# Strided heads of blocks 3 to 5 begun in the last two chunks of the block two back, and the transposes, norm and input of each block asked for one to two chunks sooner

## Chip, cores and metric

The kernel runs on one core of a Trainium2 chip. The metric is the device time of one execution in microseconds (us); the median of three runs is compared. The core's engines work side by side, each in the order of its own queue: TensorE (PE in the profile, its weight loads PEld), VectorE (DVE), ScalarE (ACT), GpSimd (POOL) and SyncE (SP), which here only starts DMA transfers.

## The reference, cut to what matters

Attention over 4 sequences of 576 positions with 8 heads of 64, then two gated feed-forward layers. Four heads are local (each query sees the 32 last keys), four are strided (each query sees the earlier keys with the same position modulo 32).

```python
scores = scale * np.matmul(q, k.transpose(0, 1, 3, 2))
mask_local = (rel >= 0) & (rel < stride)                      # heads 0 to 3
mask_strided = (rel >= 0) & (pos[None, :] % stride == pos[:, None] % stride)   # heads 4 to 7
attn = softmax(where(mask, scores, -1e9)); x = attn @ v       # 2304 tokens x 512
xn = x / sqrt(mean(x*x) + 1e-6) * rms_g                       # first layer, 512 -> 1536 -> 512
x = (silu(xn @ w_gate) * (xn @ w_val)) @ w_out
out = ((x @ w_a) * (x @ w_b)) @ w2_out                        # second layer, the same sizes
```

## The kernel before

**Blocks and chunks.** The 2304 tokens are cut into six blocks of 384 (96 positions of each sequence), `t` = 0 to 5. The first layer runs block by block. Inside a block the 1536 hidden channels are cut into twelve chunks of 128, `fc` = 0 to 11. A chunk is 12 matmuls for the gate (`g_ps`), 12 for the value (`v_ps`) and 12 for the output of the chunk before (`y`); each product is made of three matmuls, of a high and a low part of both operands (L475 to L477). Between them ACT makes `sg` (Silu, L737), DVE `h` = `sg` times the value (L747), ACT the high part of `h` (L489) and POOL or DVE its low part (L490). The second layer follows the sixth block and is not touched.

**Attention beside it.** While block `t` is on PE, the attention of block `t + 1` is worked out by the other engines, in steps that `attention_slot` (L600) asks for after each chunk's gate matmuls. The steps of the strided heads need no PE. `lq` (L209) loads the queries `qs_t` and sets the score tile `S`; `ls0` to `ls3` load the keys of a head into a `kv` buffer (L217); `sqk<head><row>` multiplies on POOL (L232) and sums on DVE (L235); `ssub`, `sexp`, `snorm` are the softmax; `lv0` to `lv3` load the values; `spv<head><row>` multiplies on POOL (L265) and sums on DVE (L268) into `xs_t`. Then `xst0` and `xst1` turn `xs_t` around on PE (L388), `xstc` copies the result on ACT (L397), `sq2` and `sq3` square it (L409) and add the squares (L415). `rms` sums the squares with a matmul (L421), `rinv` takes the root (L425) and the reciprocal on DVE (L427), and `xp0` to `xp3` make the block's input: `xn` on DVE (L433), its high part on ACT (L437) and its low part on DVE for blocks 2 and 4 and on POOL for blocks 1, 3 and 5 (L438). These are the operands of the next block's first matmuls.

**Which chunk asks for what.** The list of strided steps has 42 entries for blocks 2 to 5: `lq`, 16 for the scores, 3 for the softmax, 16 for the values, and the six `xst0 xstc0 xst1 xstc1 sq2 sq3`. It is spread evenly over chunks 0 to 9; `rms` and `rinv` are asked for in chunk 10 and the four `xp` in chunk 11. The local heads have a list of their own (`LOCAL`, L51): `qk` on PE (L280), then mask (L298), maximum (L307), exponential (L317 or L320), norm, transposes and values.

**Who sets the order.** Steps are emitted in program order, and the compiler's planner then orders each engine's queue by that priority and by its own estimate of when an instruction is ready. An engine that the planner sees idle takes later work early. What holds work back is a buffer: `qs_t` and `xs_t` share one buffer (tag `qx`, `bufs=1`), `S` has one, `kv` has three, `prod` two.

**Block 5.** Beside block 5 there is no attention to make. Its place in SBUF is taken by the forms of the second layer's weights (`convert_forms`): raw halves are loaded (L106), decoded by ACT and DVE (L129, L134, L137), split into high and low parts by ACT and POOL (L142, L143), summed (L656 to L659) and stored. The tiles of this pool lie over those of the attention's pool, so the first raw loads wait for the last reader there.

```python
for fc in range(NFC):
    ...                                    # gate and value matmuls of chunk fc of block t
    if nxt is not None:
        attention_slot(nxt, fc)            # steps of block t + 1
    if prev is not None:
        emit_y(*prev)                      # output matmuls of the chunk before
```

Of the kernel before, what the change touches and what calls it, by code (L numbers as in the profile page):

```python
# [10 lines left out]
F32 = mybir.dt.float32  # L11
# [7 lines left out]
B, H, S, D = 4, 8, 576, 64  # L19
# [3 lines left out]
NB = S // PB  # L23
NTB = B * PB
NM = S // W
NFC = FF // 128
NCC = DM // 128
# [27 lines left out]


FUSED = ["  F", "   ", "   ", "F  ", "FFF", "FFF"]
# [17 lines left out]
def fused_kernel(ctx: ExitStack, tc: tile.TileContext, qtl, ktl, vl, qs, ks, vs, cst, w1, w2, out):  # L75
# [79 lines left out]
    def run(steps):  # L155
        for f in steps:
            f()
# [13 lines left out]
    def attention(t, pool, psum, banks):  # L171

        L = 3 * (t + 1)
        G = {0: 4, 1: 2}.get(t, 1)
        KX, KB = (12 * D, 2) if t < 2 else (NM * D, 3)
        st = {}
        steps = {}

# [27 lines left out]
        def heads(g):  # L206
            return slice(g * G, g * G + G)

        def load_q():  # L209
            q_t = pool.tile([128, 4, 3, D], F32, tag="qx", name="qs_t", bufs=1)  # L210
            nc.sync.dma_start(q_t, qs[:, :, 3 * t:3 * t + 3, :])
            st["qs"] = q_t
            st["S"] = pool.tile([128, 4, 3, 6 if t < 2 else NM], F32, tag="S", name="S_t", bufs=1)
            nc.vector.memset(st["S"], NEG)

        def load_kv(src, key, g):
# [7 lines left out]
        def product(n):  # L224
            pr = pool.tile([128, KX], F32, tag="prod", name="prod", bufs=2)
            return pr[:, :G * n * D].rearrange("p (g n d) -> p g n d", g=G, d=D)
# [32 lines left out]
        def spv(g, mm):  # L259
            def f():  # L260
                n = 3 * t + mm + 1
                if "xs" not in st:
                    st["xs"] = pool.tile([128, 3, 4, D], F32, tag="qx", name="xs_t", bufs=1)
                pr = product(n)
                st["pvm"] = nc.gpsimd.tensor_tensor(  # L265
                    pr, st["vs", g][:, :, :n, :],
                    st["S"][:, heads(g), mm, :n, None].to_broadcast([128, G, n, D]), op=ALU.mult)
                st["pvr"] = nc.vector.tensor_reduce(st["xs"][:, mm, heads(g), :],  # L268
                                                    pr.rearrange("p g n d -> p g d n"), axis=X, op=ALU.add)
            return f  # L270
# [194 lines left out]
        qk_steps = [f"sqk{g}{mm}" for g in range(ng) for mm in range(3)]  # L465
        pv_steps = [f"spv{g}{mm}" for g in range(ng) for mm in range(3)]
        for lst, ld in ((qk_steps, "ls"), (pv_steps, "lv")):
            for g in reversed(range(ng)):
                lst.insert(max(0, 3 * (g - 1)), f"{ld}{g}")
        steps["strided"] = ["lq"] + qk_steps + ["ssub", "sexp", "snorm"] + pv_steps + ["xst0", "xstc0", "xst1", "xstc1", "sq2", "sq3"]  # L470
        return steps


# [5 lines left out]
    def mm_in(ps, w, sel, x):  # L479
        for cc in range(NCC):  # L480
            c = slice(cc * 128, (cc + 1) * 128)
            mm3(ps, w[:, sel, 0, c], w[:, sel, 1, c], x[cc][:, 0], x[cc][:, 1], cc == 0, cc == NCC - 1)
# [13 lines left out]
    psum = one.enter_context(tc.tile_pool(name="psum", bufs=1, space=bass.MemoryType.PSUM))  # L496
# [11 lines left out]
    pool = apool.enter_context(tc.tile_pool(name="early", bufs=1))  # L508
# [15 lines left out]
    def load_late(which):  # L524
        raw.update(zip(which, load_pair(w1, which, pool)))
# [67 lines left out]
    def load_wo(t, fc):  # L593
        wt = wo[t, fc] = wo_tile()
        nc.sync.dma_start(wt.rearrange("p a n -> p (a n)").bitcast(F32), wod[fc])


    local = [dict(enumerate(order.split("|"))) for order in LOCAL]

    def attention_slot(steps, fc):  # L600
        st = steps["strided"]
        n_sl = 10
        part = st[len(st) * fc // n_sl:len(st) * (fc + 1) // n_sl] if fc < n_sl else []
        part += local[min(t, 1)].get(fc, "").split()
        part += ["rms", "rinv"] * (fc == n_sl) + [f"xp{cc}" for cc in range(4)] * (fc == n_sl + 1)
        for n in part:
            steps[n]()


# [69 lines left out]
    def x_forms(g):  # L679

        b = {}

        def load():
            for n, (j, (t, k)) in enumerate({"11": (0, 0), "12": (1, 0), "22": (1, 1), "21": (0, 1)}.items()):
                b[j] = slab[n // 2][:, n % 2 * 2 * NTB:(n % 2 + 1) * 2 * NTB].rearrange("p (c n) -> p c n", c=2)
                nc.sync.dma_start(b[j], x2d[2 * g + t, k])

        def form(p, src):
            f = xf[p] = slab[FORM_SLAB[p]][:, :4 * NTB].rearrange("p (a c n) -> p a c n", a=2, c=2)
            parts(src, f[:, 0], f[:, 1], nc.gpsimd if p in (3, 4, 7) else nc.vector)  # L690

        def less(dst, x, y):
            nc.vector.tensor_tensor(b[dst], b[x], b[y], op=ALU.subtract)


        return {1: [load],
                2: [lambda: form(1, b["11"]), lambda: less("11", "12", "11")],
                5: [lambda: form(5, b["11"]), lambda: less("12", "22", "12"), lambda: less("11", "22", "11"),
                    lambda: form(6, b["11"]), lambda: form(2, b["21"])],
                6: [lambda: form(7, b["12"])],  # L700
                7: [lambda: form(3, b["22"])],
                8: [lambda: less("21", "21", "11"), lambda: form(4, b["21"])]}

    x0 = x_forms(0)
    prev = None
    for t in range(NB):
        if t == 1:
            apool.close()
            pool = apool.enter_context(tc.tile_pool(name="attn", bufs=1))
        if t == NB - 1:  # L710
            apool.close()
            cpool.close()
            pool = p2.enter_context(tc.tile_pool(name="forms", bufs=1, reuse_waits="tile"))
            early = [f for k in (4, 5, 0, 1, 2, 3) for f in convert_forms(k, k < 4)]
        nxt = attention(t + 1, pool, psum, itertools.cycle(["att"])) if t + 1 < NB else None
        x = [xt[t, cc] for cc in range(NCC)]
        for fc in range(NFC):
            if t > 0 and fc == 0:
                load_wo(t, 0)
            g_ps = psum.tile([128, 512], F32, tag="gv", name="g_ps", bufs=3)  # L720
            mm_in(g_ps[:, :NTB], gv[fc], 0, x)
            v_ps = psum.tile([128, 512], F32, tag="gv", name="v_ps", bufs=3)
            mm_in(v_ps[:, :NTB], gv[fc], 1, x)
            if t == 0 and fc + 1 < NFC:
                with gate(fc + 1):
                    convert1(fc + 1)
                if fc + 2 == NFC:
                    load_late([(NFC - 2, 2), (NFC - 1, 2)])
            if t == NB - 1:
                slab[fc] = wgt.tile([128, 4 * DM], F32 if fc in (0, 1, 11) else F32R, tag="gv", name="slab", bufs=NFC)  # L730
                run(early[len(early) * fc // NFC:len(early) * (fc + 1) // NFC])
                for k in [k for k in x0 if k <= fc]:
                    run(x0.pop(k))
            sg = tmp("sg")
            if t == 0:
                nc.vector.tensor_tensor(sg, g_ps[:, :NTB], ri0, op=ALU.mult)
            nc.scalar.activation(sg, sg if t == 0 else g_ps[:, :NTB], AF.Silu)  # L737
            if fc == 1 and t > 0:
                evac_y(t - 1)
            if nxt is not None:  # L740
                attention_slot(nxt, fc)
            if prev is not None:
                emit_y(*prev)
            if t > 0 and fc + 1 < NFC:
                load_wo(t, fc + 1)
            h = tmp("h")
            nc.vector.tensor_tensor(h, sg, v_ps[:, :NTB], op=ALU.mult)  # L747
            hl[t, fc] = split(h, engine(HLO0[fc] if t == 0 else HLO[t]))
            if t == 0:
                wt = wo[0, fc] = wo_tile()  # L750
                with gate(fc + 1):
                    run(conversion(raw.pop((fc, 2)), wt, pool, engine(WLO[fc][2]), LOW[fc][2]))
                nc.sync.dma_start(wod[fc], wt.rearrange("p a n -> p (a n)").bitcast(F32))
                if fc % 2:
                    load_units(1)
                if fc == NFC - 3:
                    load_late([(NFC - 1, 0), (NFC - 1, 1)])
            prev = (t, fc)
# [7 lines left out]
    psum = p2.enter_context(tc.tile_pool(name="psum2", bufs=1, space=bass.MemoryType.PSUM, reuse_waits="tile"))  # L766
# [132 lines left out]
    steps = [(ps, g, p) for ps in (range(0, 3), range(3, 6)) for g in range(NB // 2) for p in ps]  # L899
# [99 lines left out]
```

## Time and profile before

| what | value |
|---|---|
| median of 3 runs | 1017.31 us (1016.94 to 1019.99) |
| the profiled execution's own time | 1017.75 us |
| its span, first to last instruction | 1016.0 us |
| PE busy | 961.8 us (95%) |
| DVE, POOL, ACT busy | 640.6, 543.2, 427.5 us |
| mean granted TensorE clock | 0.973 |
| blocks 1 to 5 of the first layer | from 141 to 596 us of the span |

Shares of busy time are averages over stages with different limits. What ends PE's idle time, stretch by stretch, tells more than they do. The granted clock is given in parts of the full 2.4 GHz; 0.5 is the lower level, 1.2 GHz.

### The profile page before, as it was taken

The page shows a single profiled execution, that of the slowest core. Times are in us where ns is not written, and L with a number is a line of the kernel's source. Part 1 is how long each engine was busy: PE and PEld are TensorE (multiplying, and loading weights), DVE is VectorE, ACT ScalarE, POOL GpSimd, SP SyncE. Part 2 cuts the span into 40 slices and gives each one's busy share as a digit, 9 for nine tenths or more (in the row PEclk, how much of TensorE's full clock was granted, in tenths as well). Part 3 has the DMA queues.
Part 4 walks back from the last instruction along what each step waited for, and adds up shares of the span by engine and source line. Part 5 has one row for each costly group of instructions (what it writes and reads, how often), then busy time and mean ns, then how long its engine had stood idle before and what let it go on. Part 6 is the DMA issues. An engine that isn't in the chain of part 4 may idle for free.

```text
span 1016.0 us, 14355 instructions
## 1 busy us (share of the span) xinstructions
PE 961.8 (95%) x5438; PEld 908.7 (89%) x5438; DVE 640.6 (63%) x869; ACT 427.5 (42%) x832; POOL 543.2 (53%) x416
## 2 busy tenths in 40 slices
PE   6898799999999999699959999999999999999998
PEld 5698699998998999599959999999999998999996
DVE  5699957538808674978366536866856556455444
ACT  4878645236223523342366552644533432222110
POOL 4588747456729776678365722656651533223111
PEclk6999999999999999899989999999999999999999
DMA  9953357435534453242299946599894783772701
GB/s 349 407 208 122 107 188 279 130 115 171 165 113 151 154 173 122 88 142 81 90 341 367 372 156 252 197 392 394 311 376 190 286 301 136 272 308 105 271 40 63
DMA packets 57365, 215.57 MB, mean 212 GB/s; under 512 B 5968, under 2 KB 14544, under 8 KB 51664
## 3 DMA queue, kind: packets, MB, share of 16 engines
q1 hardware_dynamic: 57296, 214.66, 58.0%
q8 instruction: 43, 0.70, 0.3%
q14 instruction: 26, 0.21, 0.1%
HBM read 172.17 MB, written 42.47 MB: 211 GB/s over the span
## 4 chain that ended last, share of the span: by engine, by line
PE 69%; DVE 13%; ACT 6%; POOL 4%; issue 4%; DMA 3%; SPq 0%; DVEq 0%; POOLq 0%; ACTq 0%
PE o L878 4%; PE o L880 4%; PE o L879 4%; PE Y L822 3%; PE Y L824 3%; PE Y L823 3%; PE g_ps L476 3%; PE v_ps L475 3%; PE v_ps L476 3%; PE g_ps L475 3%; PE y L476 3%; PE v_ps L477 3%; PE g_ps L477 3%; PE y L475 3%; PE y L477 3%
## 5 line engine op out<-in xcount | busy, mean ns | idle before, releaser
L143 POOL TENSOR_TENSOR hl<-c,hl 128x384 fp32r<-128x384 f32 x72 | 77.4, 1076 | 190.8 <-ACT hl L142 180.2
L232 POOL TENSOR_TENSOR prod<-kv_t,qs_t 128x512 f32<-128x512 f32 (+12 forms) x57 | 106.8, 1894 | 18.9 <-DVE S_t L235 6.1
L475 PE MATMUL g_ps<-xx,gv 128*128 128x384 f32 x288 | 100.6, 349 | 12.7 <-DVE h L747 11.4
L490 POOL TENSOR_TENSOR hl<-h,hl 128x384 fp32r<-128x384 f32 x58 | 63.6, 1096 | 79.4 <-ACT hl L489 78.0
L475 PE MATMUL v_ps<-xx,gv 128*128 128x384 f32 x288 | 98.6, 343 | 7.2 <-ACT sg L737 4.8
L476 PE MATMUL g_ps<-xx,gv 128*128 128x384 f32 x288 | 100.4, 349 | 4.9 <-DVE xx L438 4.9
L477 PE MATMUL g_ps<-xx,gv 128*128 128x384 f32 x288 | 99.6, 346 | 0.0
L477 PE MATMUL y<-hl,wo 128*128 128x384 f32 x288 | 99.0, 344 | 0.0
L829 DVE TENSOR_TENSOR c<-c,Y 128x384 f32<-128x384 f32 x108 | 59.1, 551 | 63.2 <-PE Y L824 57.8
L476 PE MATMUL y<-hl,wo 128*128 128x384 f32 x288 | 98.3, 341 | 0.3 <-DVE hl L490 0.2
L265 POOL TENSOR_TENSOR prod<-kv_t,S_t 128x512 f32<-128x512 f32 (+12 forms) x57 | 85.4, 1511 | 23.8 <-issue 7.8
L476 PE MATMUL v_ps<-xx,gv 128*128 128x384 f32 x288 | 98.0, 340 | 0.0
L477 PE MATMUL v_ps<-xx,gv 128*128 128x384 f32 x288 | 97.6, 339 | 0.0
L268 DVE TENSOR_REDUCE xs_t<-prod 128x64 f32<-128x448 f32 (+17 forms) x57 | 85.4, 1517 | 13.2 <-POOL prod L265 13.0
L747 DVE TENSOR_TENSOR h<-sg,v_ps 128x384 f32<-128x384 f32 x72 | 39.0, 542 | 80.7 <-PE v_ps L477 62.3
L475 PE MATMUL y<-hl,wo 128*128 128x384 f32 x288 | 85.4, 344 | 0.6 <-ACT hl L489 0.6
L878 PE MATMUL o<-slab,hl 128*128 128x512 f32 x216 | 84.6, 392 | 1.0 <-DVE slab L887 0.5
L879 PE MATMUL o<-slab,hl 128*128 128x512 f32 x216 | 84.6, 392 | 0.0
L880 PE MATMUL o<-slab,hl 128*128 128x512 f32 x216 | 83.4, 394 | 0.0
L142 ACT CAST hl<-c 128x384 fp32r<-128x384 f32 x72 | 36.9, 513 | 109.5 <-DVE c L859 109.3
L822 PE MATMUL Y<-slab,form 128*128 128x384 f32 x216 | 73.1, 338 | 0.1
L824 PE MATMUL Y<-slab,form 128*128 128x384 f32 x216 | 73.1, 338 | 0.0
(142 smaller groups left out, 2546.5 us busy)
## 6 DMA issues: line engine op xcount, KB each, us to landing
form<-formd SPq DMA_DIRECT2D x32, 1792.0 KB, 10.6
wo<-wod SPq DMA_DIRECT2D x60, 512.0 KB, 3.7
raw<-in_w SPq DMA_DIRECT2D x42, 512.0 KB, 5.5
gv_raw<-in_w SPq DMA_DIRECT2D x30, 512.0 KB, 10.1
formd<-form SPq DMA_DIRECT2D x6, 1792.0 KB, 9.1
formd<-forms SPq DMA_DIRECT2D x6, 1792.0 KB, 11.1
slab<-x2d SPq DMA_DIRECT2D x24, 384.0 KB, 5.8
wod<-wo SPq DMA_DIRECT2D x12, 512.0 KB, 2.9
```

The lines of the kernel that those rows point to most:

```text
L143: lo_eng.tensor_tensor(lo, x, hi.bitcast(F32), op=ALU.subtract)
L232: nc.gpsimd.tensor_tensor(pr, st["ks", g][:, :, :n, :], st["qs"][:, heads(g), mm:mm + 1, :].to_broadcast([128, G, n, D]), op=ALU.mult)
L265: st["pvm"] = nc.gpsimd.tensor_tensor(pr, st["vs", g][:, :, :n, :], st["S"][:, heads(g), mm, :n, None].to_broadcast([128, G, n, D]), op=AL ...
L268: st["pvr"] = nc.vector.tensor_reduce(st["xs"][:, mm, heads(g), :], pr.rearrange("p g n d -> p g d n"), axis=X, op=ALU.add)
L475: nc.tensor.matmul(out_ps, w_hi, x_hi, start=start, stop=False)
L476: nc.tensor.matmul(out_ps, w_hi, x_lo, start=False, stop=False)
L477: nc.tensor.matmul(out_ps, w_lo, x_hi, start=False, stop=stop)
L822: nc.tensor.matmul(bank(n), hi, x[p][:, 0, c], start=begins and c == 0, stop=False, skip_group_check=not begins)
L824: nc.tensor.matmul(bank(n), lo, x[p][:, 0, c], start=False, stop=c == 1, skip_group_check=not begins)
L878: nc.tensor.matmul(o, h[:, 0, cols], w[0], start=n == 0, stop=False)
L879: nc.tensor.matmul(o, h[:, 0, cols], w[1], start=False, stop=False)
L880: nc.tensor.matmul(o, h[:, 1, cols], w[0], start=False, stop=n == len(chunks) - 1)
```

## The change

The list is cut in two: the 36 strided steps proper, and an `end` of six (`xst0` to `sq3`). For blocks 2 to 5 the first part is spread over chunks 0 to 7 and the end, `rms` and `rinv` are all asked for in chunk 8, the four `xp` in chunk 9. For blocks 3, 4 and 5 the first 6, 7 and 10 strided steps (`AHEAD`) are asked for earlier still, in chunks 10 and 11 of the block two back: `lq ls0 ls1 sqk00 sqk01 sqk02`, then also `ls2`, then also `sqk10 sqk11 sqk12`. Block 1 is as before. The tag `qx` and the tile `S` get a second buffer, and `kv` a fourth.

```diff
+AHEAD = {2: 0, 3: 6, 4: 7, 5: 10}
...
-        KX, KB = (12 * D, 2) if t < 2 else (NM * D, 3)
+        KX, KB = (12 * D, 2) if t < 2 else (NM * D, 4)
...
-            q_t = pool.tile([128, 4, 3, D], F32, tag="qx", name="qs_t", bufs=1)
+            q_t = pool.tile([128, 4, 3, D], F32, tag="qx", name="qs_t", bufs=1 + (t > 1))
...
-            st["S"] = pool.tile([128, 4, 3, 6 if t < 2 else NM], F32, tag="S", name="S_t", bufs=1)
+            st["S"] = pool.tile([128, 4, 3, 6 if t < 2 else NM], F32, tag="S", name="S_t", bufs=1 + (t > 1))
...
-                    st["xs"] = pool.tile([128, 3, 4, D], F32, tag="qx", name="xs_t", bufs=1)
+                    st["xs"] = pool.tile([128, 3, 4, D], F32, tag="qx", name="xs_t", bufs=1 + (t > 1))
...
-        steps["strided"] = ["lq"] + qk_steps + ["ssub", "sexp", "snorm"] + pv_steps + ["xst0", "xstc0", "xst1", "xstc1", "sq2", "sq3"]
+        steps["strided"] = ["lq"] + qk_steps + ["ssub", "sexp", "snorm"] + pv_steps
+        steps["end"] = ["xst0", "xstc0", "xst1", "xstc1", "sq2", "sq3"]
...
-    def attention_slot(steps, fc):
-        st = steps["strided"]
-        n_sl = 10
-        part = st[len(st) * fc // n_sl:len(st) * (fc + 1) // n_sl] if fc < n_sl else []
-        part += local[min(t, 1)].get(fc, "").split()
-        part += ["rms", "rinv"] * (fc == n_sl) + [f"xp{cc}" for cc in range(4)] * (fc == n_sl + 1)
+    def spread(order, i, n):
+        return order[len(order) * i // n:len(order) * (i + 1) // n] if i < n else []
+
+    def attention_slot(t, steps, fc):
+
+        order = steps["strided"]
+        xps = [f"xp{cc}" for cc in range(NCC)]
+        if t == 1:
+            part = spread(order + steps["end"], fc, 10) + local[0].get(fc, "").split()
+            part += ["rms", "rinv"] * (fc == 10) + xps * (fc == 11)
+        else:
+            part = spread(order[AHEAD[t]:], fc, 8) + local[1].get(fc, "").split()
+            part += (steps["end"] + ["rms", "rinv"]) * (fc == 8) + xps * (fc == 9)
         for n in part:
+            steps[n]()
+
+    def ahead_slot(t, steps, i):
+        for n in spread(steps["strided"][:AHEAD[t]], i, 2):
             steps[n]()
...
-        nxt = attention(t + 1, pool, psum, itertools.cycle(["att"])) if t + 1 < NB else None
+        nxt = after or attention(t + 1, pool, psum, itertools.cycle(["att"])) if t + 1 < NB else None
+        after = None
...
-                attention_slot(nxt, fc)
+                attention_slot(t + 1, nxt, fc)
+            if t + 2 in AHEAD and AHEAD[t + 2] and fc >= NFC - 2:
+                after = after or attention(t + 2, pool, psum, itertools.cycle(["att"]))
+                ahead_slot(t + 2, after, fc - NFC + 2)
```

## Rows read from the trace of the kernel before

**Rows 1.** The page, part 1: busy time of each engine.

```profile
PE 961.8 (95%) x5438; PEld 908.7 (89%) x5438; DVE 640.6 (63%) x869; ACT 427.5 (42%) x832; POOL 543.2 (53%) x416
```

**Rows 2.** PE's waits, 215:305 then 305:400: us in total, times, longest.

```profile
PE g_ps L476 <- DVE xx L438: 1.4, 2, 1.0
PE att L280 <- DVE s_t L298: 0.5, 1, 0.5
...
PE att L280 <- DVE s_t L298: 2.2, 1, 2.2
```

**Rows 3.** PE's waits, 400:495 then 495:600, the same columns.

```profile
PE g_ps L476 <- DVE xx L438: 3.5, 2, 2.3
PE v_ps L475 <- ACT sg L737: 3.1, 1, 3.1
PE att L280 <- DVE s_t L298: 1.5, 1, 1.5
...
PE g_ps L475 <- DVE h L747: 9.1, 1, 9.1
PE v_ps L475 <- ACT sg L737: 1.2, 1, 1.2
```

**Rows 4.** Stretches: us, PE, PEld, DVE, ACT, POOL busy, clock, DMA share, GB/s.

```profile
193.70:216.00 22.30, 22.30 (x153) 21.50 (x152) 1.66 (x3) 6.73 (x14) 6.03 (x6) 1.00 0.34 115
476.80:499.10 22.30, 22.30 (x141) 21.60 (x140) 6.62 (x7) 7.37 (x14) 5.62 (x6) 1.00 0.25 92
...
312.90:327.80 14.90, 12.68 (x79) 11.88 (x78) 14.90 (x20) 6.40 (x11) 13.60 (x10) 0.89 0.46 147
402.20:439.50 37.30, 29.17 (x154) 26.56 (x153) 35.48 (x41) 14.58 (x25) 26.29 (x13) 0.91 0.31 99
...
528.90:536.40 7.50, 5.31 (x20) 5.31 (x21) 6.17 (x10) 4.19 (x9) 2.64 (x3) 0.59 1.05 424
469.30:476.80 7.50, 7.50 (x56) 7.13 (x55) 7.09 (x6) 2.02 (x4) 7.37 (x6) 1.00 0.21 71
```

**Rows 5.** Timelines of DVE, POOL, SP, block 1: start, us, operation, [idle before].

```profile
189.10 1.20 DVE L268 TENSOR_REDUCE xs_t<-prod 128x64 f32<-128x576 f32 x1 [0.31 <-POOL prod L265]
...
216.56 6.55 POOL L232 TENSOR_TENSOR prod<-kv_t,qs_t 128x640 f32<-128x640 f32 x4 [0.78 <-DMA qs_t<-in_qs]
...
189.10 0.33 SPq L220 DMA_DIRECT2D kv_t<-in_ks  x1
...
212.81 0.55 SPq L211 DMA_DIRECT2D qs_t<-in_qs  x1
```

**Rows 6.** Lines L737, L433, L438, L232: durations ns min/median/max, first and last start.

```profile
L737 ACT ACTIVATE sg<-g_ps x60: 468/492/495, 149.5 to 587.8; 128x384 f32<-128x384 f32 x60
...
L433 DVE SCALAR_TENSOR_TENSOR xn<-x_t,cst_sb,rinv x20: 603/634/2745, 139.0 to 503.4; 128x384 f32<-128x384 f32 x20
...
L438 DVE TENSOR_TENSOR xx<-xn,xx x8: 546/1678/2729, 229.7 to 418.2; 128x384 fp32r<-128x384 f32 x8
...
L232 POOL TENSOR_TENSOR prod<-kv_t,qs_t x57: 722/1848/2799, 8.0 to 438.9; 128x512 f32<-128x512 f32 x7, 128x768 f32<-128x768 f32 x7, 128x640 f32<-128x640 f32 x6, 128x448 f32<-128x448 f32 x4
```

**Rows 7.** Timelines of DVE and POOL at the start of block 4.

```profile
403.08 4.56 DVE L433 SCALAR_TENSOR_TENSOR xn<-x_t,cst_sb,rinv 128x384 f32<-128x384 f32 x3
...
412.39 2.73 DVE L438 TENSOR_TENSOR xx<-xn,xx 128x384 fp32r<-128x384 f32 x1
...
412.08 2.62 POOL L232 TENSOR_TENSOR prod<-kv_t,qs_t 128x1152 f32<-128x1152 f32 x1 [2.09 <-DVE S_t L235]
```

**Rows 8.** SP's own waits, 140:545: us in total, times, longest.

```profile
SPq L220 <- POOL prod L232: 34.9, 12, 8.0
...
SPq L106 <- DVE xn L433: 7.8, 1, 7.8
```

**Rows 9.** The chain that ended last, 495:545: start, us, what.

```profile
505.23 4.23 DMA raw<-in_w
...
531.22 0.40 ACT sg L737
```

More of the change, by code (lines that the diff above doesn't have):

```diff
@@ L704, in fused_kernel @@
     x0 = x_forms(0)
-    prev = None
+    prev = after = None
     for t in range(NB):
```

## The prediction

> **What bounds the kernel now.** I read the page first, then PE's waits by stretches, then the busy time of all engines in the same stretches, then the timelines of DVE, POOL and SP around the places found. The page says that PE is busy for 95% of the span while DVE and POOL have 63% and 53% [rows 1], so what is to be won is PE's idle time and its time at the lower clock. The waits show where that lies beside blocks 1 to 5: around the four block boundaries. Into block 2, PE waited 1.4 us for the low part of the block's input (`xx` on DVE) and 0.5 us for a mask; into block 3, 2.2 us for a mask [rows 2]. Into block 4 it waited 3.5 us for `xx`, 1.5 us for a mask, 3.1 us for `sg`; into block 5, 9.1 us for an `h` and 1.2 us for an `sg` [rows 3].
>
> The stretches tell why. In the last three chunks of a block DVE does nearly nothing: 1.66 of 22.3 us at the end of block 1, 6.62 of 22.3 at the end of block 4, and POOL 6.03 and 5.62. Right behind, DVE is full: 14.90 of 14.90 us into block 3, 35.48 of 37.3 into block 4 [rows 4]. The work is thus not too much, it stands in the wrong place. That full helpers alone don't stop PE is seen in the middle of block 4: with DVE at 7.09 and POOL at 7.37 of 7.5 us PE was busy throughout [rows 4]. PE stops only where what is late is its own operand.
>
> Why the gap is there is seen in block 1. The last sum of the strided values ended at 189.10 + 1.20 = 190.3 us, and SP issued the first keys of the next block at 189.10. But the queries of the next block were issued only at 212.81, and POOL began its products at 216.56 on their landing [rows 5]. The queries share their one buffer with `xs_t`, which is read by the transposes, and these are asked for in chunks 8 and 9. So the planner does pull the next block's work forward, by as much as the buffer lets it: it ran from 216.56 beside the norm and the `xn` of the coming block, and DVE had both at once.
>
> A chunk takes (587.8 − 149.5)/59 = 7.43 us, from the first to the last of 60 `sg` [rows 6].
>
> **The change part by part.** No arithmetic goes and none is added; the strided products, sums and loads are the same in number. Costs come from order alone.
>
> *Second buffers for `qs_t`/`xs_t` and `S`, a fourth for `kv`, and the steps ahead.* The wait that held the queries until 212.81 is gone: their buffer is free when the scores of the block before are done, in mid-block. Asked for in chunk 10, the steps can run from chunk 10 on, and by what the planner did with the keys (issued at 189.10, 27 us ahead of their first use at 216.56) from the end of the values on, 190.3. That is up to 26 us before 216.56, in a gap where POOL has 22.3 − 6.03 = 16.3 us free and DVE 20.6 [rows 4]. The work ahead is 3 products for block 3, 3 for block 4, and 6 for block 5, at most 6 × 2.8 = 16.8 us of POOL [rows 6]: it fits. It costs nothing there as long as the products don't stand in front of something that PE waits for; below I charge for that.
>
> *Transposes, norm, input.* `rinv` moves from chunk 10 to 8 and the `xp` from 11 to 9, 14.9 us sooner. The waits for `xx` and for masks queued behind the `xn` and `xx` on DVE are then covered. Term by term:
>
> Into block 2: 1.4 + 0.5 = 1.9 us [rows 2].
>
> Into block 3: 2.2 us [rows 2], and the clock. The granted clock was 0.89 over 14.9 us [rows 4], so 0.11 × 14.9 = 1.6 us of full-speed work were lost; that is the lower level for some 3.3 us, following the wait. Sum 3.8 us.
>
> Into block 4: 3.5 + 1.5 = 5.0 us for `xx` and mask, 3.1 us for `sg` [rows 3], and (1 − 0.91) × 37.3 = 3.4 us of clock [rows 4], which I split evenly over the two waits. The first part, 5.0 + 1.7 = 6.7 us, goes with the earlier `xp`. The second, 3.1 + 1.7 = 4.8 us, is an `sg` held up on ACT behind an exponential of the local heads, itself late on the full DVE. Emptying DVE helps it, but the order on ACT stays the planner's. Bounds 0 and 4.8; no row is nearer to either, so the middle, 2.4. Sum 9.1 us.
>
> Into block 5: 9.1 + 1.2 us [rows 3] and clock: 0.41 × 7.5 = 3.1 us lost in 528.9:536.4 [rows 4], of which about 1.1 us fall on the 2.2 us in which PE was idle anyway; 2.0 are left. Together 12.3 us. Here the chain runs unbroken from the first raw load at 505.23 through the decoding of the weights to the late `sg` at 531.22 [rows 9], and that load stood 7.8 us at the head of SP's queue for the last `xn` [rows 8]. With the `xn` two chunks sooner this wait is gone. Bounds 0 (the decoding is slow wherever it begins) and 12.3; I take the 7.8 us of the wait and the clock that went with the stall, 9.8 us.
>
> The sum of gains is 1.9 + 3.8 + 9.1 + 9.8 = 24.6 us.
>
> *What it may add.* The transposes, the squares, the sum of squares and its matmul are now asked for in one chunk instead of three, while POOL, which adds the squares, is busy with products from the block after. PE takes its queue in order: behind the matmul of the norm stand the chunk's own matmuls. The trace of before has no wait there to read; a square's sum that finds a product in front is late by up to 2.8 us [rows 6]. Bounds for four boundaries 0 and 11.2 us; mostly PE's queue is some matmuls behind the planner's idea and hides it, so I take 3 us, about a quarter.
>
> The profiled execution took 1017.75 us, 0.44 over the median of 1017.31. 1017.75 − 24.6 + 3.0 = 996.2 us.
>
> **The rivals.**
>
> *Block 5's stall stays.* If it is the order of the decoding steps on ACT and not the late load that holds `sg`, the 9.8 us are not won: 1006 us. For it: raw loads, table and sums stand in a row with nothing between. Against: SP's wait of 7.8 us is right ahead of the chain [rows 8].
>
> *DVE and POOL in each other's way.* A product of 2.62 us began on POOL at 412.08, and the `xx` that DVE began at 412.39 took 2.73 us, until 0.42 us after that product's end [rows 7]; the shortest `xx` took 0.546 us, the shortest `xn` 0.603 against 2.745 for the longest [rows 6]. If all four `xn` and four `xx` of blocks 2 and 4 meet a product each, they take 4 × 2.75 + 4 × 2.73 = 21.9 us instead of 4.6; these 17.3 us eat the 14.9 that were given, and the 1.9 and 6.7 us into blocks 2 and 4 are not won: 996.2 + 8.6 = 1005 us. Against: three `xn` in a row took 4.56 us even on the full DVE [rows 7]. The Trainium skill (SBUF — State Buffer, "Who interferes with whom") states this as a rule: a DVE instruction with two SBUF inputs fully blocks while a GpSimd instruction that reads SBUF holds the shared ports. By that rule, it is this rival whenever the planner puts products beside the `xp`; the trace of before agrees on single instructions.
>
> *Nothing moves.* The planner already runs ahead; if it pulls nothing into the gap and the `xp` stay behind the queue on DVE, the time stays at 1017 us. Against: the keys at 189.10 and the products on the very landing of the queries [rows 5].
>
> *Slower: SP's queue.* SP issues in order. Loads of keys stood there for a POOL product for 34.9 us in 12 waits, the longest 8.0 [rows 8]. With 10 or 11 loads and queries pulled a block ahead, a load that waits for a `kv` buffer may stand in front of `wo`, the weights of the output matmuls. Each `wo` late by 8.0 us stops PE by as much once its spare buffers are used up; from 4 such on, 32 us, it decides: 996.2 + 32 = 1028 us, slower from 3 waits plus a little (24.6 − 3.0 = 21.6 us to be used up). Against: PE has no wait for `wo` now, and the fourth `kv` buffer eases the queue.
>
> **How the numbers follow.** Forecast (996 us, own range 987 to 1003) 0.56; block 5 stays 0.15; ports 0.09; nothing moves 0.08; SP's queue 0.12. The likeliest is taken, 996. With everything at its upper bound, gains are 1.9 + 3.8 + 11.5 + 12.3 = 29.5 us and no new wait, 988 us; the low end is 986. The high end takes in the first two rivals and half their shortfall together: 1011. Outside lie the last two, 0.20. A difference under 0.3%, 3 us, can't be told from none here. Faster holds the first three: 0.80; same 0.08; slower 0.12.
>
> **What would show it.** In the stretches at the ends of blocks 1 to 4, DVE and POOL should be busy for more than half; the queries of blocks 3 to 5 issued before the transposes of the block ahead; the last `xn` of each block done some 12 us before its first matmul; no wait for `xx` or `s_t` at PE into blocks 2 to 4; the clock at 1.00 through blocks 2 to 4; the first raw load issued without a wait, and the 9.1 us wait at most 2. The forecast is wrong if the waits for `h` or `sg` come back in another chunk, if PE waits at the transposes (L388) or the norm's matmul (L421), or if `y` waits for `wo`.

## The result, and the profile after

The changed kernel takes 1029.69 us (median of 4 runs, 1028.56 to 1030.91), the kernel before 1017.12 (1015.94 to 1019.99): the ratio is 1.0124 [1.0105, 1.0142]. It is 12.6 us slower, and the prediction, 996 us and 986 to 1011, had the wrong direction. The profiled execution took 1029.51 us, its span is 1027.6.

The page, part 1, of the kernel after, beside [rows 1]:

```profile
PE 965.6 (94%) x5438; PEld 914.4 (89%) x5438; DVE 625.0 (61%) x869; ACT 429.5 (42%) x831; POOL 541.0 (53%) x416
```

Stretches of the kernel after, in the columns of [rows 4]: blocks 1 to 5, the end of the strided values beside block 1, and the 22.4 us behind the norm of block 2's input.

```profile
141.00:608.00 467.00, 435.40 (x2608) 423.40 (x2609) 267.76 (x337) 190.44 (x373) 290.83 (x213) 0.96 0.50 174
...
190.00:210.00 20.00, 20.00 (x138) 19.23 (x137) 9.79 (x12) 6.21 (x11) 20.00 (x14) 1.00 0.52 169
...
216.00:238.40 22.40, 14.73 (x83) 14.06 (x84) 22.40 (x25) 9.11 (x15) 12.27 (x10) 0.77 0.39 127
```

The first and the last of them in the kernel before, where PE ran nearly unhindered in the last:

```profile
141.00:596.00 455.00, 430.56 (x2608) 417.29 (x2609) 283.31 (x338) 191.14 (x379) 294.12 (x214) 0.98 0.52 180
...
216.00:238.40 22.40, 20.41 (x117) 18.98 (x116) 18.45 (x22) 8.66 (x13) 14.96 (x10) 1.00 0.33 106
```

The first rows account for the whole loss. The same 2608 matmuls took 467.0 us instead of 455.0: PE idle 31.6 instead of 24.4 us, 7.2 more, and 4.8 us more of busy time at a mean clock of 0.96 instead of 0.98. The run-ahead did what it should beside block 1: POOL is full at the end of the values, where [rows 4] showed it at 6.03 of 22.3. But in the last stretch DVE is full for all 22.4 us, PE busy for 14.73 instead of 20.41, and the clock at 0.77 instead of 1.00. In the kernel before this stretch reaches over the boundary into block 2; in the changed one it still lies in the last chunks of block 1.

PE's waits in blocks 1 to 5 of the kernel after (141:610; total, times, longest), and of the kernel before (141:596; its largest, 9.1 us for an `h`, is in [rows 3]):

```profile
PE g_ps L478 <- DVE h L765: 10.7, 2, 6.0
PE att L423 <- POOL sq L417: 7.2, 4, 2.4
PE g_ps L478 <- ACT sg L752: 6.4, 5, 2.5
PE att L282 <- DVE s_t L300: 4.8, 1, 4.8
PE att L282 <- ACT rms_t L427: 2.0, 3, 0.7
...
PE g_ps L476 <- DVE xx L438: 4.9, 4, 2.3
PE v_ps L475 <- ACT sg L737: 4.8, 3, 3.1
PE att L280 <- DVE s_t L298: 4.5, 4, 2.2
```

The waits for the low part of `xx` (L440 now, L438 before), 4.9 us, are gone; that much was right. New are a wait of 1.4 to 2.4 us at the norm's matmul (L423) in each of four blocks and 2.0 us behind it for the root. Waits for masks, `sg` and `h` are not fewer than before, 4.8, 6.4 and 10.7 us in place of 4.5, 4.8 and 9.1; they stand in other places, 6.0 us of those for `h` in block 5.

PE's timeline after, block 1: start, duration, operation, idle time before it and what ended it.

```profile
211.12 0.49 PE L390 MATMUL att<-cst_sb,xs_t 128*128 128x128 f32 x3
214.50 0.91 PE L423 MATMUL att<-sq,ones 128*128 128x384 f32 x2 [2.37 <-POOL sq L417]
...
221.81 0.33 PE L479 MATMUL v_ps<-xx,gv 128*128 128x384 f32 x1
221.98 0.33 PE L480 MATMUL v_ps<-xx,gv 128*128 128x384 f32 x1
...
230.11 1.97 PE L282 MATMUL att<-k_t,q_t 128*64 128x64 f32 x16 [4.81 <-DVE s_t L300]
234.18 0.69 PE L478 MATMUL g_ps<-xx,gv 128*128 128x384 f32 x1 [2.11 <-ACT sg L752]
234.67 0.52 PE L479 MATMUL g_ps<-xx,gv 128*128 128x384 f32 x1
234.99 0.52 PE L480 MATMUL g_ps<-xx,gv 128*128 128x384 f32 x1
```

In PE's timeline of the kernel before, the first transposes (L388 there), which were asked for in chunk 8 already, came 0.65 us later, the second 1.17 us later, and the norm's matmul (L421) at 219.23, without a wait:

```profile
212.29 0.49 PE L388 MATMUL att<-cst_sb,xs_t 128*128 128x128 f32 x3
219.23 0.81 PE L421 MATMUL att<-sq,ones 128*128 128x384 f32 x2
```

What holds the mask stands in DVE's timeline after; the last two rows are from the kernel before:

```profile
216.87 2.54 DVE L429 RECIPROCAL rinv<-rms_t 128x384 f32<-128x384 f32 x1
219.33 0.49 DVE L765 TENSOR_TENSOR h<-sg,v_ps 128x384 f32<-128x384 f32 x1
...
222.99 2.25 DVE L435 SCALAR_TENSOR_TENSOR xn<-x_t,cst_sb,rinv 128x384 f32<-128x384 f32 x2
...
225.62 0.60 DVE L435 SCALAR_TENSOR_TENSOR xn<-x_t,cst_sb,rinv 128x384 f32<-128x384 f32 x1
226.15 1.23 DVE L270 TENSOR_REDUCE xs_t<-prod 128x64 f32<-128x640 f32 x1
227.29 0.55 DVE L440 TENSOR_TENSOR xx<-xn,xx 128x384 fp32r<-128x384 f32 x1
227.76 1.83 DVE L311 TENSOR_TENSOR s_t<-s_t,lmx 128x384 f32<-128x384 f32 x1
229.51 0.55 DVE L300 SCALAR_TENSOR_TENSOR s_t<-att,cst_sb 128x384 f32<-128x384 f32 x1
...
235.57 0.54 DVE L765 TENSOR_TENSOR h<-sg,v_ps 128x384 f32<-128x384 f32 x1
...
220.69 2.55 DVE L427 RECIPROCAL rinv<-rms_t 128x384 f32<-128x384 f32 x1
225.15 1.14 DVE L433 SCALAR_TENSOR_TENSOR xn<-x_t,cst_sb,rinv 128x384 f32<-128x384 f32 x2
```

From 222.99 on, DVE does three `xn` of the next block, a sum of run-ahead values, an `xx` and a step of the local softmax before the mask at 229.51 that PE had stood for since 225.30, and no `h` between 219.33 and 235.57. The mask isn't one of the running chunk: the scores at L282 are those of block 3's local heads, which the program asks for only in block 2 and the planner had pulled forward. They take turns with the norm in the one `att` bank, so PE waits until DVE has read the last ones. On ACT it looks the same:

```profile
215.45 0.58 ACT L427 ACTIVATE rms_t<-att,eps_sb 128x384 f32<-128x384 f32 x1 [0.77 <-PE att L423]
216.05 1.28 ACT L752 ACT_TABLE_LOAD   x1
217.34 0.49 ACT L752 ACTIVATE sg<-g_ps 128x384 f32<-128x384 f32 x1
...
223.63 0.52 ACT L439 CAST xx<-xn 128x384 fp32r<-128x384 f32 x1 [3.26 <-DVE xn L435]
...
226.79 1.28 ACT L319 ACT_TABLE_LOAD   x1
...
232.35 1.28 ACT L752 ACT_TABLE_LOAD   x1 [2.21 <-DVE xx L440]
233.64 0.49 ACT L752 ACTIVATE sg<-g_ps 128x384 f32<-128x384 f32 x1
```

Between two `sg` stand 16.3 us, more than two chunks of 7.43, taken up by casts of the next block's input, waits for DVE and two table switches. Such a gap is not new: in the kernel before, 17.3 us lie between the `sg` at 225.22 and the next at 242.54, across the boundary. What differs is what PE had to do meanwhile. The gap before, then the gap after:

```profile
225.70:242.50 16.80, 14.81 (x94) 13.06 (x92) 15.26 (x19) 5.80 (x10) 12.51 (x8) 1.00 0.29 95
...
217.80:234.10 16.30, 9.38 (x60) 8.88 (x60) 16.30 (x18) 5.63 (x10) 7.84 (x6) 0.80 0.40 126
```

At the boundary PE went on with output matmuls of the old block and with the first gate and value matmuls of the new one, 14.81 of 16.80 us at full clock. In mid-block it was busy for 9.38 of 16.30, at a mean clock of 0.80.

### The profile page after: what moved, and what is told of

It reads as the page before. It is cut to its first block, busy times and chain, and to the rows that moved or that the text cites. A ratio compares the mean times of both kernels' runs of the same rounds, so it can differ in the third digit from the quotient of the medians.

```text
span 1027.6 us, 14359 instructions
## 1 busy us (share of the span) xinstructions
PE 965.6 (94%) x5438; PEld 914.4 (89%) x5438; DVE 625.0 (61%) x869; ACT 429.5 (42%) x831; POOL 541.0 (53%) x416
## 4 chain that ended last, share of the span: by engine, by line
PE 69%; DVE 10%; POOL 7%; DMA 6%; ACT 4%; issue 4%; SPq 0%; POOLq 0%; DVEq 0%; ACTq 0%
PE o L896 4%; PE o L898 4%; PE o L897 4%; PE g_ps L478 4%; PE Y L840 4%; PE g_ps L479 4%; PE Y L842 4%; PE Y L841 3%; PE g_ps L480 3%; PE y L478 3%; PE y L479 3%; PE y L480 3%; PE v_ps L478 3%; PE v_ps L479 3%; PE v_ps L480 3%
## 5 line engine op out<-in xcount | busy, mean ns | idle before, releaser
L478 PE MATMUL g_ps<-xx,gv 128*128 128x384 f32 x288 | 103.5, 360 | 20.6 <-DVE h L765 13.0
L493 POOL TENSOR_TENSOR hl<-h,hl 128x384 fp32r<-128x384 f32 x58 | 66.2, 1144 | 80.1 <-ACT hl L492 72.8
L480 PE MATMUL g_ps<-xx,gv 128*128 128x384 f32 x288 | 102.2, 355 | 0.0
L479 PE MATMUL g_ps<-xx,gv 128*128 128x384 f32 x288 | 101.9, 354 | 0.0
L478 PEld LDWEIGHTS g_ps<-xx,gv 128*128 128x128 f32 x288 | 57.9, 201 | 23.6 <-DVE h L765 13.8
L237 DVE TENSOR_REDUCE S_t<-prod 128x8 f32<-128x512 f32 (+12 forms) x57 | 53.8, 948 | 35.6 <-POOL prod L234 35.4
```

What stands on the lines that cost most here:

```text
L478: nc.tensor.matmul(out_ps, w_hi, x_hi, start=start, stop=False)
L479: nc.tensor.matmul(out_ps, w_hi, x_lo, start=False, stop=False)
L480: nc.tensor.matmul(out_ps, w_lo, x_hi, start=False, stop=stop)
L493: lo_eng.tensor_tensor(hl[:, 1], h, hl[:, 0].bitcast(F32), op=ALU.subtract)
```

## The experiments

Times are medians; ratios are to the kernel before on the same chip, which took 1017.84 to 1019.16 us in the five sets.

**Which part is slower.** Each of the three parts by itself. First the buffers alone, in the kernel before:

```
-KX, KB = (12 * D, 2) if t < 2 else (NM * D, 3)
+KX, KB = (12 * D, 2) if t < 2 else (NM * D, 4)
 qs_t, S_t, xs_t: bufs=1  ->  bufs=1 + (t > 1)
```

> The kernel before, with the second buffers for qs_t/xs_t and S and the fourth kv buffer alone. Crowding (the loss comes from transposes, squares, norm matmul and root asked for in one chunk): not slower than before, 1005 to 1017 us, and no wait at the norm's matmul. Run-ahead (the loss comes from work of later blocks that the buffers let in front of masks, xn and h on DVE at the boundaries): slower, 1022 to 1032 us, with waits of 4 us and more for s_t or h at two or three boundaries.

1013.57 us, 0.9945 [0.9928, 0.9962]. Next the earlier end with the old buffers and no steps ahead (`AHEAD = {2: 0, 3: 0, 4: 0, 5: 0}`):

> The changed kernel with no steps ahead and the old number of buffers: only the end, norm and input asked for sooner. Crowding: PE waits of about 3 us around the norm's matmul at each of four boundaries, 13 us, less what the earlier input gives back into blocks 2 to 4; slower than before, 1018 to 1026 us. Run-ahead: faster than before, 1000 to 1010 us, since the input comes sooner and nothing new stands in front of it.

1038.88 us, 1.0202 [1.0180, 1.0224], more than either theory gave, and without any run-ahead in the way. Then the changed kernel with the end back in its old place:

```
+part = spread(order[AHEAD[t]:] + steps["end"], fc, 10) + local[1].get(fc, "").split()
+part += ["rms", "rinv"] * (fc == 10) + xps * (fc == 11)
```

> The changed kernel with its buffers and its steps ahead, but the end spread with the rest over chunks 0 to 9, the norm in chunk 10 and the input in chunk 11 as before. Crowding: no wait at the norm's matmul, 1000 to 1015 us. Run-ahead: as slow as the changed kernel or nearly, 1022 to 1032 us.

1013.32 us, 0.9944 [0.9925, 0.9963]. Two things follow. The loss is all in the earlier end. And the steps asked for ahead add nothing to the buffers (1013.3 against 1013.6): the planner pulls the work forward by itself as soon as a buffer lets it. With the buffers alone SP issued the queries of block 3 at 171.34, in the changed kernel at 169.42. Then the norm and the input one chunk later each:

```
-part += (steps["end"] + ["rms", "rinv"]) * (fc == 8) + xps * (fc == 9)
+part += steps["end"] * (fc == 8) + ["rms", "rinv"] * (fc == 9) + xps * (fc == 10)
```

> The changed kernel with the norm one chunk after the end (chunk 9 instead of 8) and the input in chunk 10 instead of 9; all else as changed. Crowding: the waits at the norm's matmul and the two behind it (13.5 us in sum over four boundaries) go, 1012 to 1019 us. Run-ahead: the waits at the boundaries stay, 1024 to 1030 us.

1016.24 us, 0.9973 [0.9956, 0.9991]: by the ratios one chunk gives back 0.0151 of the 0.0180 that lie between the changed kernel and the one with its buffers and the old end.

**Is it the crowding of transposes, squares and norm in one chunk?** That was my first theory. If so, the same norm in chunk 8, with the transposes and squares spread out before it, would not cost:

```
+part = spread(order[AHEAD[t]:], fc, 7) + local[1].get(fc, "").split()
+part += end[:2] * (fc == 6) + end[2:] * (fc == 7) + ["rms", "rinv"] * (fc == 8) + xps * (fc == 9)
```

> The changed kernel, with the norm still in chunk 8 and the input still in chunk 9, but the transposes a chunk and more ahead of them (values over chunks 0 to 6, first transpose in chunk 6, second and the squares in chunk 7). Crowding (norm asked for beside its own squares is what loses the time; a sooner input is good by itself): 997 to 1006 us, no wait at the norm's matmul, no wait for xx. Rival, a sooner input buys nothing (the boundary waits are for masks and h on a full DVE, whatever the input does): 1010 to 1018 us, as with the input one chunk sooner.

1030.23 us, 1.0121 [1.0104, 1.0137]: as slow as the change, and above both ranges. The theory fell, though the test is not clean. PE's timeline of this kernel:

```profile
208.13 0.49 PE L390 MATMUL att<-cst_sb,xs_t 128*128 128x128 f32 x3
214.93 0.91 PE L423 MATMUL att<-sq,ones 128*128 128x384 f32 x2 [1.43 <-POOL sq L417]
```

The first transposes came 13 us sooner than in the changed kernel (193.75 for 206.78) and the second 3.0 (208.13 for 211.12), the norm's matmul not: it stays at 214.93 with its wait for the squares. The same, one chunk later throughout (transposes in 7 and 8, norm 9, input 10):

> The same spacing of the steps as before the change, all one chunk sooner (first transpose in chunk 7, second and squares in 8, norm in 9, input in 10), with the changed buffers and steps ahead. Crowding: 1003 to 1010 us, between the two. A sooner input buys nothing: 1010 to 1018 us.

1016.05 us, 0.9978 [0.9965, 0.9990], as without the staging. Splitting the root and the reciprocal over chunks 8 and 9:

```
+part += (steps["end"] + ["rms"]) * (fc == 8) + (["rinv"] + xps) * (fc == 9)
```

> The changed kernel with the root and reciprocal moved from chunk 8 to 9; the norm's matmul stays in chunk 8 beside the squares. If PE's wait at the norm's matmul for the squares is what loses (1.4 to 2.4 us at each of four boundaries, with the clock's fall behind it): 1024 to 1030 us. If it is the root with its table load on ACT, in front of the chunk's sg: the waits at L423 stay but those for rms_t and sg behind it go, 1015 to 1022 us.

1044.88 us, 1.0263 [1.0248, 1.0279], the slowest of all and above both ranges. Here PE has no wait at the norm's matmul at all, and waits for masks (141:620) nearly four times those of the changed kernel. First that wait, then ACT's timeline:

```profile
PE att L282 <- DVE s_t L300: 18.3, 6, 4.1
...
221.50 0.58 ACT L427 ACTIVATE rms_t<-att,eps_sb 128x384 f32<-128x384 f32 x1 [4.04 <-PE att L423]
...
228.74 0.51 ACT L439 CAST xx<-xn 128x384 fp32r<-128x384 f32 x1 [6.65 <-DVE xn L435]
...
237.82 0.52 ACT L319 ACTIVATE s_t<-s_t 128x384 f32<-128x384 f32 x1 [5.21 <-DVE s_t L311]
...
239.65 0.49 ACT L752 ACTIVATE sg<-g_ps 128x384 f32<-128x384 f32 x1
```

ACT takes its queue in order: it stood 6.65 us at a cast for an `xn`, then 5.21 us at an exponential for a mask, and the chunk's own `sg` came at 239.65, 18.2 us after the root. So the wait at the norm's matmul is not what the loss hangs on: without it, the work behind the norm still stood in the way.

**Block 5's raw load.** In the kernel before, the raw halves of block 5 got a pool of their own, so that their load need not wait for the last `xn`:

```
+rawp = one.enter_context(tc.tile_pool(name="rawp", bufs=1, side="right"))
-    pool.tile([128, 2, DM], U32, tag="raw", name="raw", bufs=2)
+    (p2c if spare else rawp).tile([128, 2, DM], U32, tag="raw", name="raw", bufs=2)
```

> The kernel before, with the raw weight halves of block 5 in space of their own (second stage's raw halves moved as well), so that their first loads don't wait for the last xn. If the late first load makes the 9.1 us wait into block 5 (the forecast's term of 9.8 us): that wait at most 2 us, 1007 to 1010 us. If the order of the decoding steps in front of sg and h makes it: a wait of 6 us or more stays, 1014 to 1019 us.

1014.25 us, 0.9959 [0.9944, 0.9975]. PE's waits of this kernel, 500:620:

```profile
PE g_ps L475 <- ACT sg L738: 5.4, 1, 5.4
```

The `h` of 9.1 us [rows 3] is gone, but `sg` now makes PE wait 6.2 us (5.4, and 0.8 at a value matmul) where it was 1.2. The run also gave the raw halves of the second layer's own weights another place; the time behind the last `sg` of the first layer did not change by it (428.1 us, 428.2 in the kernel before).

**Are the local scores pulled along?** The next theory: the planner issues the scores of the next blocks' local heads into the boundary. They were queued behind the gate matmuls of the last chunk two blocks back:

```
+mark[t] = mm_in(g_ps[:, :NTB], gv[fc], 0, x)
+with tc.issue_after(mark[t - 2].ins) if g == 0 and t > 2 else nullcontext():
+    scores()
```

> The changed kernel, with the local heads' first scores (qk0) of blocks 3 to 5 kept behind the gate matmuls of the last chunk of the block two back in TensorE's queue, where they stood before the change; norm in chunk 8, input in chunk 9 as changed. Scores pulled along (the sooner norm frees the one PSUM bank of the attention, and the planner puts the next block's local scores right behind it, two chunks sooner, where PE waits in order for their masks on DVE): the waits of 4 to 8 us for s_t, sg and h behind the norm go, 1005 to 1016 us. Rival, norm beside the squares: the waits at the norm's matmul are what starts it, 1024 to 1030 us.

1027.04 us, 1.0086 [1.0062, 1.0110]: about 4 us of the 12.6. PE waits for no mask any more in blocks 1 to 5, but its waits for `sg` grew from 6.4 us to 13.6:

```profile
PE g_ps L483 <- ACT sg L758: 13.6, 5, 3.7
```

With norm 9 and input 10:

> The changed kernel with the norm in chunk 9 and the input in chunk 10 and the scores kept back the same way. Scores pulled along: the two waits of 5 us for s_t go, 1003 to 1010 us. Rival (norm beside the squares): nothing left to win over the same without the hold, 1014 to 1019 us.

1014.53 us, 0.9962 [0.9947, 0.9978], not apart from the same without the hold (0.9973). And with the old buffers and no steps ahead:

> Only the end, norm and input asked for sooner (old buffers, no steps ahead), with the scores kept back. Scores pulled along: 1010 to 1020 us, against 1039 us without the hold. Rival: 1033 to 1042 us.

1040.89 us, 1.0229 [1.0207, 1.0252], no better than without (1.0202). The theory fell too, as the cause of the whole: the hold gave back some 4 us in the changed kernel and nothing elsewhere. Taking the additions of the squares off POOL, which PE's wait at L423 names (`SQA = "DDPPPP"` to `"DDDDDD"`):

> The changed kernel with the additions of squares for blocks 2 to 5 on DVE in place of POOL. If POOL's additions behind products are what delays the norm's matmul, its waits of 1.4 to 2.4 us fall under 1 us each and the time by 4 to 10 us, 1019 to 1026 us. If the scores behind the norm set the loss, it changes by less than 4 us, 1025 to 1032 us.

1026.60 us, 1.0085 [1.0065, 1.0104]. PE's wait stays at the same place, now for DVE, 4.9 us instead of 7.2 (141:610):

```profile
PE att L423 <- DVE sq L417: 4.9, 4, 2.1
```

The squares' place on POOL is thus worth some 4 us, and the rest is elsewhere.

**Norm and input apart.** The line of `norm_later` with other chunk numbers, first norm 8 and input 11:

> The changed kernel with the norm still in chunk 8 but the input asked for in chunk 11, as before the change. Input in mid-block (ACT's casts of the input wait in order for xn on DVE, and the chunk's own sg and h stand behind them; at the block's end PE has the output matmuls of two chunks to go on with): 1012 to 1020 us, with no wait of 2 us and more for sg or h between the norm and the boundary. Norm and root in mid-block (their wait and table loads alone): 1024 to 1031 us.

1023.03 us, 1.0039 [1.0021, 1.0058], between the two ranges. Norm 8, input 10:

> The changed kernel with the norm in chunk 8 and the input in chunk 10. Input in mid-block: between the changed kernel and the one with the input in chunk 11, 1016 to 1026 us. Norm and root in mid-block: 1024 to 1031 us, the same as the other two.

1017.36 us, 0.9993 [0.9975, 1.0011]. Norm 9, input 11:

> The changed kernel with the norm in chunk 9 and the input in chunk 11. Input in mid-block: as with the norm in chunk 10, 1008 to 1014 us. Norm and root in mid-block: as with norm in 9 and input in 10, 1014 to 1018 us.

1012.79 us, 0.9945 [0.9930, 0.9960]. In all three the transposes and squares are in chunk 8, as in the changed kernel. With the new buffers, then, the ratio is 0.9944 with norm 10 and input 11, 0.9945 with the transposes in 8 and the norm in 9, 1.0039 with the norm in 8, and 1.0124 when the input goes from 11 to 9 as well: steps of 0.0094 for the norm from 9 to 8 and 0.0085 for the input, together the whole way from the buffers' gain to the result. Neither the transposes nor norm 9 cost anything there. PE's timeline with norm 9 and input 11 has the second transposes where the changed kernel has them, and no wait at the norm's matmul:

```profile
211.24 0.49 PE L390 MATMUL att<-cst_sb,xs_t 128*128 128x128 f32 x3
217.49 0.81 PE L423 MATMUL att<-sq,ones 128*128 128x384 f32 x2
```

The two steps hold for this path only. With input 10 the norm's step from 9 to 8 is 0.0020 (0.9973 to 0.9993, not clear of noise), and with norm 8 the input's step from 10 to 9 is 0.0131. Norm 8 and input 9 together are what costs most; norm 9 with input 9 was not run. DVE's timeline with norm 8 and input 11:

```profile
223.31 0.55 DVE L300 SCALAR_TENSOR_TENSOR s_t<-att,cst_sb 128x384 f32<-128x384 f32 x1
...
225.22 0.54 DVE L765 TENSOR_TENSOR h<-sg,v_ps 128x384 f32<-128x384 f32 x1
...
230.68 2.67 DVE L435 SCALAR_TENSOR_TENSOR xn<-x_t,cst_sb,rinv 128x384 f32<-128x384 f32 x3
```

Here the mask and the chunk's next `h` (225.22) stand ahead of the `xn` (230.68); in the changed kernel they stood behind them (229.51 and 235.57 after 222.99). At L423 PE still waits:

```profile
PE att L423 <- POOL sq L417: 7.5, 4, 2.7
```

Last, ACT's casts of `xx` on POOL in the changed kernel, to see whether ACT's queue or DVE's carries the loss (`(nc.gpsimd.tensor_copy if t > 1 else nc.scalar.copy)(xx[:, 0], xn)`):

> The changed kernel with the casts of the input (xx high, blocks 2 to 5) on POOL in place of ACT, so that no sg stands behind them. Input in mid-block by way of ACT's queue: the waits for sg behind the norm go, 1015 to 1023 us. By way of DVE's queue (h behind xn, and masks) or of the norm and root: 1025 to 1034 us.

1037.82 us, 1.0193 [1.0161, 1.0224], slower than either theory gave. There is a new wait of 8.1 us, at 329.66 to 337.81, for a step of the local softmax on DVE (`lsm`, L332). In 318:340 DVE was busy for 21.97 of 22.00 us and POOL for 18.37, so the run made these two fuller and does not say which queue carries the loss.

**A version that beats both?** Norm 9, input 11 with the squares on DVE (`"DDDDDD"`):

> The changed kernel with the norm in chunk 9, the input in chunk 11 and the additions of squares for blocks 2 to 5 on DVE. It puts together what did no harm: 1008 to 1013 us. If the additions on DVE stand behind its other work there, 1013 to 1017 us.

1013.80 us, 0.9964 [0.9951, 0.9978]. The same norm and input with the old buffers and nothing ahead:

> The norm in chunk 9 and the input in chunk 11, with the old number of buffers and no steps ahead. If the gain of 0.55% at this place is the buffers' alone: 1015 to 1020 us, as the kernel before. If the norm one chunk sooner gains by itself: 1010 to 1014 us.

1020.73 us, 1.0024 [1.0012, 1.0037]. The earlier norm alone wins nothing; the gain of norm 9 and input 11 is that of the buffers. In the traces it is less simple. ACT's last `sg` of the first layer began at 587.84 in the kernel before, at 583.69 with the buffers alone, at 579.14 with norm 9 and input 11, but the rest of the kernel then took 430.9 us instead of 427.6 with the buffers alone, with new waits at the passage to the second layer. The best versions lie at 0.9944 to 0.9945 and can't be told apart, so the simplest is the one to keep: the buffers alone, some 5.6 us faster than before.

## Why the prediction was wrong, point by point

**The run-ahead: right, in mechanism.** The forecast's "last three chunks" of block 1, 193.7 to 216.0, are its chunks 7 to 9: their `sg` began at 195.57, 202.84 and 210.41, those of chunks 10 and 11 at 217.00 and 225.22. The queries of blocks 3, 4 and 5 were issued at 169.42, 211.64 and 309.69 (before, 212.81 for block 3 [rows 5]), POOL filled the end of the values, and the buffers that allow it are worth 0.55%. That it costs nothing where it lands held as well (`ahead_only`). It was not what the forecast was made of. At the end of block 4 the gap did not fill: DVE had 3.88 and POOL 9.12 us to do in 439.5:499.1, as block 5's attention, the last one, had been done by then (its last product on POOL began at 395.08).

**The failed step: "14.9 us sooner", and that the waits "are then covered".** What each boundary gave in the two profiled executions, together -12.2 us, can be read from ACT's `sg` of chunk 7 in blocks 1 to 5, which began at 195.57, 283.96, 372.62, 470.44 and 563.87 in the kernel before and at 194.90, 293.31, 390.43, 481.40 and 575.40 in the changed one:

| into block | gain forecast, us | gain measured, us | `rinv` sooner by, counted from chunk 7, us | DVE busy in the 22.4 us from the norm's matmul on: before, after |
|---|---|---|---|---|
| 2 | 1.9 | -10.0 | 3.2 | 20.38, 21.20 |
| 3 | 3.8 | -8.5 | 6.1 | 21.36, 20.16 |
| 4 | 9.1 | 6.9 | 4.6 | 22.15, 17.07 |
| 5 | 9.8 | -0.6 | 4.6 | 12.09, 12.93 |

Into block 4 the forecast nearly came true: DVE was less full there than before, and PE's 5.0 us for `xx` and a mask went. Into blocks 2 and 3, where DVE was about as full as before, the change lost 18.5 us. The step has two faults.

First, asking two chunks sooner did not bring the norm two chunks sooner. Into block 2 the transposes moved by 0.65 and 1.17 us, and the norm's matmul moved from 219.23 to 214.50, with PE waiting for it. `rinv` began at 216.87 instead of 220.69 in the kernel before, 3.8 us sooner (3.2 counted from chunk 7), and the first `xn` at 222.99 instead of 225.15, 2.2 us sooner. At no boundary was `rinv` more than 6.1 us sooner. `staged_two_sooner` shows the same from the other side: with its first transposes 13 us sooner the norm's matmul is at 214.93.

Second, covering the waits at the start of a block was bought with the block's own chunks. The terms 1.9, 3.8 and 9.1 us took away the waits for `xx` and masks and asked nothing of what the moved work would stand in front of. DVE and ACT take their queues in order; in mid-block the `rinv`, `xn`, casts and `xx` stand before the running chunk's `sg` and `h`, and before the masks of scores pulled forward, and PE, which needs these, was busy for 9.38 of 16.30 us between two `sg`. `input_last`, `input_ten` and `norm_nine_input_last` show that the place of the input and of the norm decide. That it is the order on DVE and ACT is read from the timelines, not shown by an undisturbed experiment; `cast_on_pool` was to settle it and did not. For it speak the runs that took one wait away: without the wait at the norm's matmul (`root_later`) or without the masks (`scores_held`) PE stood for other results of the same two engines.

**What it may add.** The new wait at the norm's matmul, 3 us with a bound of 11.2, measured 7.2 us at L423 and 2.0 behind it for the root: within the bounds, nearer the upper. What was left out is that masks, `sg` and `h` would be waited for in mid-block (4.8, 6.4 and 10.7 us above) as much as before at the boundaries, and the lower clock behind these waits, the 4.8 us of busy time above. The forecast itself named a wait at that matmul and the return of `h` and `sg` as signs that it was wrong, and both came.

**Into block 5: right place, about twice too large.** In the changed kernel the load stood 15.1 us at the head of SP's queue for the last `xn`, not less, and was issued at 509.60; counted from chunk 7 of block 4 that is 6.1 us sooner than before (504.78), not 14.9, and `h` still held PE for 6.0. Taken away by itself in `raw_apart`, the late load gave 0.41%, about 4 us, against a term of 9.8 with the bounds 0 and 12.3. The 6.2 us at `sg` that stayed go with the order of the decoding: ACT's timeline of that run has steps of the decoding between the `sg` at 516.73 and the late one at 528.15. The rival "block 5's stall stays" was half true.

**The rivals.** Nothing moves: false. SP's queue: PE has no wait for `wo` in the kernel after; the slower side came by another way, on which no chance stood. DVE and POOL in each other's way was not tried by itself, but the traces speak against it as the cause: DVE's 869 instructions took 625.0 us in all, 640.6 before [rows 1], and the eight `xx` that it makes 5.0 us instead of 13.4. Long single `xn` still occur (1.61 us for one at 232.17, where the shortest took 0.603 [rows 6]).

**The switch of tables around the root.** In the rows of ACT a switch costs 1.29 us: the root ends at 216.03, the load of 1.28 runs from 216.05, `sg` begins at 217.34. The Trainium skill (ScalarE: Activation LUTs, "What ACT_TABLE_LOAD costs") has 1.283 us for the load and 1.38 us for a drain, some 2.66 us together. The load agrees with the rows; the drain does not show here, and the measurement decides.

**Open.** Why norm 8 with input 11 (1.0039) is slower than with input 10 (0.9993), while with norm 9 it is the other way about (0.9945 against 0.9973). The traces (1023.07 and 1020.13 us) only tell where: with norm 8 the last `sg` of the first layer began at 589.49 with input 11 and at 590.41 with input 10, and the rest took 431.7 and 427.6 us, so their difference arose behind that `sg` and not in mid-block. What the place of the input does to that passage no run shows.

## What to carry to other kernels

A chain that is late at the start of a block is not simply asked for sooner: look first at what stands behind it in each in-order queue at the new place, and whether the matmul engine has other work there; here PE was busy for 14.81 of 16.80 us of a gap at a boundary and for 9.38 of 16.30 of one in mid-block. Give the planner buffers before an order: second buffers for two tiles and a fourth for a third gave 0.55%, the steps written out ahead nothing more. Read off how far each instruction of the chain really moved before the gain of a move is booked. And a wait that PE shows is only the last of a row: when one was taken away, the next result of the same full engines held PE instead.

## What was not expected of the hardware

A RECIPROCAL of 128x384 on DVE took 2.54 us where an `h` of the same size took 0.49 to 0.55, so one step of the norm holds DVE's queue as long as five of the chunk's own. And waits are paid for twice: in 216:238.4 of the changed kernel the granted clock was 0.77, and after PE had stood 4.81 us and then 2.11 us, matmuls of 128x384 began 0.32 us apart (234.67 and 234.99) where they had begun 0.17 apart (221.81 and 221.98), that is at the lower level of 1.2 GHz instead of 2.4.
